# Linear attention with a channel mix on one core: pairs of heads share the handling of their maxima, q's exponentials are taken in one piece, the last tile is written in halves, and the instruction order is new

## The chip, the cores and the metric

The kernel runs on one core of a Trainium2 chip. The metric is the device time of one execution in microseconds (us), and lower is better. The engines of the core work side by side, each through its own list of instructions in order: TensorE (PE, matrix products), VectorE (DVE), ScalarE (ACT), GpSimd (POOL), and SyncE (SP), which here only issues transfers. They wait for one another through semaphores. SBUF is the on-chip memory. PSUM is where matrix products land.

## The reference, cut to what matters

Two operations follow each other. The first is a linear attention for 8 batches of 8 heads, 576 tokens each, head size 64. Its features are exponentials of a projection and of its negative, with the largest magnitude of each token taken off.

```
def phi(x):
    proj = einsum('bhsd,df->bhsf', x, w_phi)                 # 64 -> 128 features
    proj = proj - max(abs(proj), axis=-1, keepdims=True)
    return concatenate([exp(proj), exp(-proj)], axis=-1)     # 256 features
q_p, k_p = phi(q), phi(k)
kv  = einsum('bhsf,bhsd->bhfd', k_p, v);   z = sum(k_p, axis=2)
num = einsum('bhsf,bhfd->bhsd', q_p, kv);  den = einsum('bhsf,bhf->bhs', q_p, z)
attn = num / (den + 1e-06)
```

Its output, with the heads side by side as 512 columns, goes through a channel mix. That mix blends each token with the one before it and applies three products.

```
xk = mu_k * x + (1 - mu_k) * x_prev;  xr = mu_r * x + (1 - mu_r) * x_prev
k = maximum(xk @ w_k, 0)              # 512 -> 1024
out = sigmoid(xr @ w_r) * ((k * k) @ w_v)
```

## The kernel before

Heads are handled in pairs, one head in partitions 0 to 63 and the other in 64 to 127, so there are 32 pairs, four to a batch. A pair's tokens are cut into nine groups: eight are handled by the pair itself, and the ninth (the "edge") is handled for all pairs of a batch together. Nothing about the order is left to a scheduler. Each step is a named operation, and a long list of words called ORDER says in which sequence they are put out; since each engine works in order, this fixes the sequence on each engine. A word such as `mc5/ACT` puts the step mc of pair 5 on ScalarE, `kp1:0+2@2` puts kp of pair 1 into PSUM buffer 0 after two filler products, and a trailing `.d` marks the landing of a transfer.

The steps of one pair n, in the order of the data:

```
kp, qp   PE    projections of k and q (8 products each) into PSUM, 128 x 1024
rk, rq   DVE   per token the negated largest magnitude: nmk, nmq, 128 x 8 each
em       ACT   exp(+nmk), exp(-nmk): a factor for v (two instructions)
va, vb   POOL  v times that factor, once for each sign (some on DVE)
ea, eb   ACT   exp(+k), exp(-k), 128 x 1024 each
mh       POOL  nmq split into a high and a low bf16 part, in tile mhl (some on DVE)
mt, mc   PE, then DVE or ACT: mhl transposed, and copied out of PSUM as mT
qt       PE    q's projection once more, transposed, with mT added by selecting products
qa, qb   ACT   exp(+q), exp(-q)
kv, kc   PE, then ACT or DVE: kv and z, and their copy to SBUF
nd       PE    numerator and denominator
ra, rd   DVE   1/den, and num times it
xt or xz, xu   the result transposed (by PE, or by a transfer) and its shifted part copied
df       DVE or POOL   difference of neighbouring tokens
xa, xb   DVE   the blends xk and xr
```

For each batch the channel mix adds h (w_k product, 8 of them), rl (relu), sq (square), r (w_r product, 4), th (tanh), v (w_v product, 4), ob (product of the two branches) and so (store). An edge tile per two batches (he, rle, sqe, re, the, ve, obe, soe) does the same for the remaining tokens. The parts which the change touches:

```
        def em():
            for pn in range(2):
                nc.scalar.activation(vb[:, a, pn, 0:8, 64].rearrange("p (g r) -> p r g", r=2),
                                     s["nmk"].rearrange("p (r g) -> p r g", r=2), AF.Exp,
                                     scale=(1.0 if pn == 0 else -1.0))
        ... (cut)
        def mhx(eng):
            e = nc.vector if eng == "DVE" else nc.gpsimd
            nmv = s["nmq"].rearrange("p (a g) -> p a g", a=2)
            e.tensor_copy(mhv[:, 1, 0], nmv)
            e.tensor_tensor(mhv[:, 1, 1], nmv, mhv[:, 1, 0], op=ALU.subtract)

        def mt():
            s["pm"] = motile(("mo", "m" + N), "ps_m")
            nc.tensor.transpose(s["pm"][:, 0:64].bitcast(BF), mh, ident)

        def mc(eng):
            s["mT"] = small.tile([128, 128], BF, name="mT", bufs=BUFS["mT"])
            copy(eng, s["mT"], s["pm"][:, 0:64].bitcast(BF))
        ... (cut)
        def eq(pn):                                            # qa and qb
            def f():
                t = s[f"q{pn}"] = mid.tile([128, 2, 512], BF, name=f"q{pn}", bufs=BUFS["qpn"])
                for h in range(2):
                    nc.scalar.activation(
                        t[:, h, :].rearrange("f (g a p) -> f g a p", g=4, a=2),
                        s["qT"].rearrange("f a (g h p) -> f h g a p", g=4, h=2)[:, h],
                        AF.Exp, scale=(1.0 if pn == 0 else -1.0))
            return f
        ... (cut)
        # the edge tile's last steps
        def vm():
            s["v"] = ps = motile(("mo", f"ve{bp}"), "ps_ve")
            s["o"] = mm.tile([128, DM], FP, name="ob", bufs=BUFS["ob"])
            for fc in range(NFC):
                nc.tensor.matmul(ps, lhsT=s["kk"][:, fc, :], rhs=wv_bf[:, fc, :],
                                 start=(fc == 0), stop=(fc == NFC - 1))

        def ob():
            nc.vector.scalar_tensor_tensor(out=s["o"], in0=s["t"], scalar=1.0, in1=s["v"],
                                           op0=ALU.add, op1=ALU.mult)

        def so():
            for i in range(2):
                nc.sync.dma_start(out=out[b - 1 + i].rearrange("(p s) d -> s p d", s=R)[8 * (1 - i)],
                                  in_=s["o"][64 * i:64 * i + 64, :])
```

Of the kernel before, what the change touches and what calls it, by code (L numbers as in the profile page):

```python
# [8 lines left out]
FP = mybir.dt.float32  # L9
BF = mybir.dt.bfloat16  # L10
# [9 lines left out]
ones hk hq ident dve2 hk.d hq.d wphi wphi.d lk0.1 lk0.1.d lq0.1 lq0.1.d lv0.0/SP lv0.0.d lk0.2  # L20
lk0.2.d dve3 mus mus.d lq0.2 lq0.2.d lv0.1/POOL lv0.1.d lk0.0.d/DVE lk1.0 lk1.0.d lv0.2/SP lv0.2.d
lq0.0.d/DVE pt0.0:0+9@0 lq1.0 lq1.0.d pt0.1:1 pa0/DVE pb0/ACT tr0 lk1.2 lk1.2.d dve1 tp0.0:0+1@2
kp0:1 rt0.0 qp0:2 lq1.2 lq1.2.d rk0 ekt0.0 pt1.0:1+1@0 eme0.0 pt1.1:0 wk.0 wk.0.d pa1/ACT pb1/DVE
tr1 mhe0.0/POOL rq0 ea0 kp1:0+2@2 eb0 rk1 qp1:2+2@0 mh0/POOL wk.1 wk.1.d wk.d mt0:1 em0 tp0.1:1
mte0.0:0 ea1 mce0.0/DVE va0/POOL mc0/DVE rt0.1 pt2.0:0 pt2.1:1 pa2/DVE ekt0.1 vb0/POOL pb2/DVE tr2
eb1 qt0:1 rq1 pt3.0:1 eme0.1 lv1.0/POOL lv1.0.d pt3.1:0 qa0 qp2:0 pa3/DVE kv0:2 mh1/POOL pb3/DVE tr3
rq2 wr.0 wr.0.d qte0.0:1 kc0/ACT em1 tp0.2:2 mhe0.1/POOL qb0 mt1:0 rt0.2 kp2:0 va1/POOL rk2 mc1/ACT
ekt0.2 qp3:1 eqe0.0 vb1/POOL kp3:2+1@0 rq3 ea2 mte0.1:0 mhe0.2/POOL pt4.0:1+2@1 eb2 mce0.1/DVE kv1:1
pa4/DVE mh2/POOL rk3 qte0.1:0 eme0.2 pt4.1:1 mh3/POOL nd0:0 eqe0.1 wr.1 wr.1.d wr.d em2 mt2:0
kc1/DVE mc2/ACT pb4/DVE tr4 wv.0 wv.0.d ea3 qt1:1 ra0 rd0 pt5.0:1 va2/POOL eb3 pt5.1:0 pa5/DVE qp4:0  # L30
pb5/DVE tr5 wv.1 wv.1.d wv.d mte0.2:1 qa1 rq4 qp5:2 pt6.0:0 vb2/POOL qb1 mce0.2/DVE pa6/DVE qte0.2:1
qt2:0 lk2.0 lk2.0.d rq5 em3 eqe0.2 xt0:0 va3/POOL kp4:1 qa2 xf0/DVE xe0/DVE kv2:2 rk4 mh4/POOL mt3:0
pt6.1:1 kc2/ACT df0/POOL qb2 nd1:2 mc3/DVE pb6/DVE tr6 mt4:0 ea4 ra1 nd2:0 mc4/DVE lq2.0 lq2.0.d rd1
pt7.0:0 eb4 lv1.2/POOL lv1.2.d ra2 xt1:1 rd2 kp5:2 vb3/POOL xf1/ACT xe1/ACT qt3:1 rk5 pa7/ACT
pt7.1:1 mh5/POOL kv3:0 qa3 xa0 xt2:0 xb0 qb3 pb7/DVE tr7 xf2/ACT df1/DVE xe2/ACT tp1.0:1 kc3/DVE ea5
rt1.0 df2/POOL nd3:0+1@1 eb5 ra3 mhe1.0/POOL rd3 ekt1.0 qt4:2+4@1 xa1 xt3:0 eme1.0 mt5:1 xb1 mc5/ACT
xe3/ACT qt5:1+1@2 xa2 qa4 mte1.0:1 qp6:0 xb2 xf3/ACT qb4 df3/DVE mce1.0/DVE xa3 em5 qte1.0:1+2@0 em4
kp6:2 xb3 eqe1.0 va4/POOL rq6 r0.0:0+3@0 qa5 h0.0:1 vb4/DVE qb5 rk6 mh6/POOL kv4:0 tr2.0 tr2.0.d tr8
tr9 rl0.0/ACT vb5/POOL qp7:1 th0.0 h0.1:1 rq7 ea6 va5/POOL r0.1:0 kc4/DVE em6 rl0.1/ACT sq0.0/DVE
tr2.2 tr2.2.d tr10 tr11 kv5:0 vb6/DVE th0.1 kp7:1 eb6 mh7/DVE mt6:1 h0.2:0 rk7 sq0.1/POOL nd4:2  # L40
lk3.0 lk3.0.d mc6/DVE em7 rl0.2/DVE h0.3:1 kc5/ACT lv2.0/SP lv2.0.d vb7/POOL ea7 ra4 rd4 lv2.2/SP
lv2.2.d h0.4:0 eb7 rl0.3/DVE va7/POOL qp8:2 xt4:1 rl0.4/ACT rq8 nd5:1 va6/POOL sq0.3/ACT qt6:0
sq0.2/ACT xf4/DVE xe4/DVE tp2.0:2 lq3.0 lq3.0.d ra5 qa6 h0.5:0 rd5 sq0.4/POOL qb6 rt2.0 h0.6:1 lk4.0
lk4.0.d rl0.5/ACT kv6:1 rl0.6/DVE df4/POOL ekt2.0 qp9:0 kc6/DVE h0.7:0 rq9 sq0.5/ACT mhe2.0/POOL
mt7:1 kp8:2 rl0.7/ACT kv7:1 mc7/DVE mh8/POOL rk8 sq0.7/ACT kp9:0 sq0.6/POOL mte2.0:0 r0.2:1 eme2.0
kc7/ACT em8 xa4 nd6:1 mce2.0/ACT th0.2 xb4 v0.0:0 ea8 rk9 vb8/POOL eb8 v0.1:1 va8/POOL em9 ob0.0 ea9
ra6 so0.0 so0.0.d rd6 mh9/POOL eb9 lq4.0 lq4.0.d qte2.0:0 ob0.1 qp10:1 vb9/POOL eqe2.0 qt7:2 rq10
qp11:0 tr3.0 tr3.0.d tr12 tr13 r0.3:1 qa7 va9/POOL rq11 xt5:0 th0.3 kp10:1 mh10/POOL qb7 xe5/DVE
xt6:1 xf5/DVE rk10 kv8:0 df5/POOL tr3.2 tr3.2.d tr14 tr15 xe6/ACT mt8:0 nd7:2 kc8/ACT xf6/DVE
mc8/DVE ea10 mt9:1 xa5 qt8:0 v0.2:0 eb10 df6/DVE mc9/DVE ra7 xa6 em10 qa8 xb5 qt9:1 xb6 qb8 v0.3:1  # L50
ob0.2 va10/POOL qa9 rd7 vb10/POOL mt10:0 nd8:0 qb9 mc10/DVE ob0.3 xt7:0 ra8 kv9:2 mh11/POOL xf7/ACT
rd8 xe7/ACT kv10:1 kc9/ACT df7/DVE xz8 xz8.d qt10:0 kc10/ACT xa7 kp11:2 qa10 nd9:1 xb7 mt11:0 qb10
rk11 r1.0:1 mc11/ACT nd10:0 ra9 th1.0 rd9 r1.1:0 em11 ea11 ra10 vb11/POOL xz9 xz9.d rd10 kp12:1
th1.1 h1.0:1 rk12 va11/POOL eb11 so0.1 so0.1.d qp12:0 h1.1:0 rq12 ea12 xu8/POOL xz10 xz10.d df8/POOL
qt11:2 rl1.1/ACT rl1.0/DVE tp3.0:0 eb12 lv3.0/SP lv3.0.d h1.2:0 rt3.0 sq1.0/POOL so0.2 so0.2.d qa11
kp13:1 rl1.2/DVE mh12/POOL h1.3:1 tr4.0 tr4.0.d tr16 tr17 qb11 sq1.1/DVE sq1.2/POOL h1.4:0 rl1.3/DVE
ekt3.0 xa8 r1.2:1 eme3.0 sq1.3/DVE rl1.4/ACT qp13:0 rk13 mhe3.0/POOL kv11:2 tr4.2 tr4.2.d tr18 tr19
th1.2 em12 xu10/POOL mt12:0 h1.5:1 sq1.4/ACT xu9/POOL mc12/DVE va12/POOL kc11/DVE ea13 rq13 h1.6:0
vb12/POOL rl1.5/ACT nd11:2 rl1.6/DVE lv3.2/SP lv3.2.d em13 sq1.5/ACT qp14:0 xb8 mte3.0:1 h1.7:0 eb13
# [936 lines left out]
```

## Time and profile before

| Quantity | Value |
|---|---|
| Time, median of 3 runs | 287.51 us (286.61 to 288.0) |
| Span of the profiled execution | 286.8 us |
| DVE busy | 252.0 us, 88% of the span |
| ACT busy | 227.1 us, 79% |
| POOL busy | 156.7 us, 55% |
| Mean TensorE clock granted | 0.99 of full |

The page of the profile gives busy time for each engine, the span in 40 slices, the chain of work that ended last, and groups of equal instructions with their number, busy time and mean duration. In a group line, "out<-in" names the tile written and the tiles read, with partitions x elements and types; what stands after the second bar is the idle time of the engine just before them. The busy time of a group is less than number times mean where the ends of instructions overlap. A busy PE is not yet a full PE: its products are pipelined, so the number of products done in a stretch says more than the share of time.

### The profile page before, as it was taken

What the parts mean: (1) busy time and instruction counts of PE and PEld (TensorE: products, weight loads), DVE (VectorE), ACT (ScalarE), POOL (GpSimd) and SP (SyncE); (2) the same over time, 40 slices, a digit from 0 to 9 for tenths busy, and PEclk for the clock granted to TensorE, in tenths of its full rate; (3) what the DMA queues carried; (4) which work ended last, traced back from release to release, by engine and by line L of the source; (5) the groups of instructions that cost most, each with busy time, mean ns of one, the idle gap of its engine ahead of it and who ended that gap; (6) DMA issues with size and microseconds to landing.
All of it is one profiled execution on the core that took longest, in us unless ns stands there. A gap on an engine that the chain in (4) does not pass through costs nothing.

```text
span 286.8 us, 9054 instructions
## 1 busy us (share of the span) xinstructions
PE 267.4 (93%) x3729; PEld 154.4 (54%) x3729; DVE 252.0 (88%) x403; ACT 227.1 (79%) x488; POOL 156.7 (55%) x235
## 2 busy tenths in 40 slices
PE   6888889999999999999899989999999999999993
PEld 2556645556645656645556644565565646544541
DVE  6799999999999999999998999999999997873431
ACT  2699997999899899988879967799899979524710
POOL 8599637985567967644599446826356243300000
PEclk9799999999999999999999999999999999999998
DMA  7999989989768979995777959799831714345034
GB/s 170 219 240 248 208 196 221 193 140 197 107 86 208 209 126 199 172 209 125 230 109 103 225 160 162 173 136 187 145 49 41 197 39 98 28 94 126 22 74 110
DMA packets 65785, 42.89 MB, mean 150 GB/s; under 512 B 47120, under 2 KB 56720, under 8 KB 65744
## 3 DMA queue, kind: packets, MB, share of 16 engines
q1 hardware_dynamic: 54688, 28.19, 48.0%
q0 software_dynamic: 10912, 13.83, 27.8%
q8 instruction: 29, 0.48, 0.7%
q10 hardware_dynamic: 144, 0.29, 0.4%
q14 instruction: 12, 0.10, 0.1%
HBM read 33.62 MB, written 9.44 MB: 150 GB/s over the span
## 4 chain that ended last, share of the span: by engine, by line
PE 56%; DVE 21%; ACT 13%; DMA 4%; issue 4%; POOL 1%; SPq 0%; DVEq 0%; ACTq 0%
PE ps_h L803 16%; PE ps_v L836 12%; PE ps_r L822 8%; ACT k L600 5%; PE ps_kv L652 4%; DVE xr L728 4%; ACT q L639 4%; PE ps_nd L673 3%; DVE nmk L574 3%; DVE nmq L579 3%; DVE xk L728 3%; PE ps_q L561 2%; DMA wph_f<-in_w_phi_dram 2%; PE ps_k L561 2%; PE ps_qT L625 2%
## 5 line engine op out<-in xcount | busy, mean ns | idle before, releaser
L592 POOL TENSOR_TENSOR v<-vt,v 128x576 bf16<-128x576 f32 x57 | 72.4, 1284 | 42.9 <-ACT v L586 37.1
L639 ACT ACTIVATE q<-ps_qT 128x512 bf16<-128x512 f32 x128 | 68.1, 631 | 3.1 <-PE ps_qT L631 2.9
L600 ACT ACTIVATE k<-ps_k 128x1024 bf16<-128x1024 f32 x64 | 63.9, 1047 | 2.2 <-DVE nmk L574 1.9
L803 PE MATMUL ps_h<-xk,wk_bf 128*128 128x512 bf16 x256 | 61.6, 379 | 0.7 <-DVE mT L205 0.7
L836 PE MATMUL ps_v<-wv_bf,kk 128*128 128x512 bf16 x256 | 58.9, 379 | 0.0
L579 DVE TENSOR_REDUCE nmq<-ps_q 128x8 f32<-128x1024 f32 x32 | 38.7, 1214 | 1.9 <-PE ps_q L561 1.5
L836 PEld LDWEIGHTS <-kk 128*128 128x128 bf16 x256 | 24.2, 98 | 27.7
L574 DVE TENSOR_REDUCE nmk<-ps_k 128x8 f32<-128x1024 f32 x32 | 38.8, 1212 | 0.3 <-PE ps_k L561 0.2
L803 PEld LDWEIGHTS <-wk_bf 128*128 128x128 bf16 x256 | 22.9, 98 | 25.6 <-issue 1.3
L728 DVE SCALAR_TENSOR_TENSOR xr<-diff,mu_r_t,xs 128x576 bf16<-128x576 bf16 x32 | 33.8, 1065 | 0.0
L828 ACT ACTIVATE rt<-ps_r 128x512 bf16<-128x512 f32 x32 | 19.5, 609 | 17.6 <-PE ps_r L822 17.2
L209 ACT ACTIVATE krelu<-ps_h 128x512 bf16<-128x512 f32 x44 | 26.7, 606 | 7.6 <-PE ps_h L803 7.3
L822 PE MATMUL ps_r<-wr_bf,xr 128*128 128x512 bf16 x128 | 32.2, 379 | 0.2
L217 POOL TENSOR_TENSOR kk<-krelu 128x512 bf16<-128x512 bf16 x18 | 20.1, 1116 | 18.3 <-DVE krelu L211 11.1
L842 DVE SCALAR_TENSOR_TENSOR ob<-rt,ps_v 128x512 f32<-128x512 bf16 x32 | 21.5, 679 | 8.9 <-PE ps_v L836 7.5
L728 DVE SCALAR_TENSOR_TENSOR xk<-diff,mu_k_t,xs 128x576 bf16<-128x576 bf16 x32 | 28.1, 880 | 0.1
L685 DVE TENSOR_TENSOR x_sc<-ps_nd,rden 128x640 bf16<-128x640 f32 x32 | 26.2, 821 | 0.8
L722 POOL TENSOR_TENSOR diff<-xs 128x576 bf16<-128x576 bf16 x15 | 19.1, 1275 | 13.2 <-DVE mhl L610 4.1
L652 PEld LDWEIGHTS <-k 64*128 64x128 bf16 x1024 | 18.7, 94 | 7.0 <-issue 4.4
L561 PEld LDWEIGHTS <-qkT 64*128 64x128 bf16 x512 | 16.5, 95 | 11.0 <-issue 7.9
L652 PE MATMUL ps_kv<-v,k 64*128 64x65 bf16 x1024 | 21.9, 190 | 0.3 <-DVE x_sc L685 0.2
L673 PE MATMUL ps_nd<-kv,q 128*128 128x65 bf16 x512 | 21.4, 193 | 0.0
(102 smaller groups left out, 439.8 us busy)
## 6 DMA issues: line engine op xcount, KB each, us to landing
out_dram<-ob SPq DMA_DIRECT2D x72, 128.0 KB, 2.4
vt<-in_v_dram SPq DMA_DIRECT2D x12, 576.0 KB, 5.0
nat<-in_k_dram POOLq DMA_DIRECT2D x6, 576.0 KB, 8.5
nat<-in_q_dram POOLq DMA_DIRECT2D x6, 576.0 KB, 7.4
vt<-in_v_dram POOLq DMA_DIRECT2D x3, 576.0 KB, 11.5
wk_bf<-in_moe_w_k_dram POOLq DMA_DIRECT2D x2, 512.0 KB, 13.0
wv_bf<-in_moe_w_v_dram POOLq DMA_DIRECT2D x2, 512.0 KB, 10.1
nat<-in_k_dram POOLq DMA_DIRECT2D x3, 288.0 KB, 9.2
```

Of the source, the lines that this page charges most:

```text
L561: nc.tensor.matmul(ps[:, par, g * 128:(g + 1) * 128], lhsT=qkT[b][r, g0 + gg + g, :], rhs=wph[r, :], start=(g == 0), stop=(g == 3))
L574: nc.vector.tensor_reduce(s["nmk"], s["k"].rearrange("p a (g f) -> p (a g) f", f=128), axis=AX.X, op=ALU.max, apply_absolute_value=True, n ...
L579: nc.vector.tensor_reduce(s["nmq"], s["q"].rearrange("p a (g f) -> p (a g) f", f=128), axis=AX.X, op=ALU.max, apply_absolute_value=True, n ...
L592: (nc.vector if eng == "DVE" else nc.gpsimd).tensor_tensor(vb[:, a, pn, :, 0:64], vt[b, a // 2][:, a % 2, :].rearrange("p (s d) -> p s d", ...
L600: nc.scalar.activation(s[f"k{pn}"], s["k"].rearrange("p a (g f) -> p (a g) f", f=128), AF.Exp, scale=(1.0 if pn == 0 else -1.0))
L639: nc.scalar.activation(t[:, h, :].rearrange("f (g a p) -> f g a p", g=4, a=2), s["qT"].rearrange("f a (g h p) -> f h g a p", g=4, h=2)[:, ...
L652: nc.tensor.matmul(ps[:, hh, pn * 65:(pn + 1) * 65], lhsT=s[f"k{pn}"][r, c, :], rhs=vb[r, a, pn, 2 * g + par, :], start=(pn == 0 and c == ...
L673: nc.tensor.matmul(ps[:, bk, o * 65:(o + 1) * 65], lhsT=tail if sl < 2 else s[f"q{pn}"][:, h, G * 128:(G + 1) * 128], rhs=s["kv"][:, h, pn ...
L728: nc.vector.scalar_tensor_tensor(out=t[:, a, (b % 2) * S:(b % 2 + 1) * S], in0=s["d"], scalar=mu[:, a:a + 1], in1=xs[:, a, 0:S], op0=ALU.m ...
L803: nc.tensor.matmul(ps, lhsT=wk_bf[:, c, fc * 128:(fc + 1) * 128], rhs=xkt[bp][:, c, m0:m0 + 512], start=(c == 0), stop=(c == NDC - 1))
L822: nc.tensor.matmul(ps, lhsT=xrt[bp][:, c, m0 + ci * 128:m0 + (ci + 1) * 128], rhs=wr_bf[:, c, :], start=(c == 0), stop=(c == NDC - 1))
L836: nc.tensor.matmul(ps, lhsT=s["kk"][:, fc, ci * 128:(ci + 1) * 128], rhs=wv_bf[:, fc, :], start=(fc == 0), stop=(fc == NFC - 1))
```

## The change

From pair 4 on, two neighbouring pairs (4 and 5, 6 and 7, ...) form a unit. Their maxima land in one tile of 2 x 8 columns. One em, one mh, one mt and one mc then serve both. The transposed tile mT has room for both, because mhl had only half of its columns in use; qt selects rows 4j to 4j+3 for the pair j of the unit. Pairs 0 to 3 stay alone. The exponentials of q take all 1024 columns in one instruction, into a tile [128, 8, 128] instead of [128, 2, 512]; nd reads the same values from it. The last edge tile computes its w_v product, its ob and its store in two halves of 256 columns, and the final stores are issued by SP and ACT. The conditions by which the order was found are looser: h needs the xa of its batch alone, r the xb alone. The list ORDER is new from end to end, and with it the engine on which many steps run. The aim is less work on DVE, ACT and POOL and a shorter end.

```diff
+    ONE = 4
+        w = 1 if n < ONE else 2
+        u, c0 = (n, a) if w == 1 else (n - n % 2, a - a % 2)
+        first, last = n == u, n == u + w - 1
+        cp = cpl.setdefault(u, {})
... (cut: rk and rq write t[:, j, :] of a shared tile [128, 2, 8])
         def em():
             for pn in range(2):
-                nc.scalar.activation(vb[:, a, pn, 0:8, 64].rearrange("p (g r) -> p r g", r=2),
-                                     s["nmk"].rearrange("p (r g) -> p r g", r=2), AF.Exp,
+                nc.scalar.activation(vb[:, c0:c0 + w, pn, 0:8, 64].rearrange("p a (g r) -> p a r g", r=2),
+                                     cp["nmk"][:, 0:w, :].rearrange("p a (r g) -> p a r g", r=2), AF.Exp,
                                      scale=(1.0 if pn == 0 else -1.0))
... (cut)
-            nmv = s["nmq"].rearrange("p (a g) -> p a g", a=2)
-            e.tensor_copy(mhv[:, 1, 0], nmv)
-            e.tensor_tensor(mhv[:, 1, 1], nmv, mhv[:, 1, 0], op=ALU.subtract)
+            nmv = cp["nmq"][:, 0:w, :].rearrange("p k (a g) -> p k a g", a=2)
+            e.tensor_copy(mhv[:, 0:w, 0], nmv)
+            e.tensor_tensor(mhv[:, 0:w, 1], nmv, mhv[:, 0:w, 0], op=ALU.subtract)
... (cut: mt and mc once for each unit)
-                    nc.tensor.matmul(ps[:, par, g * 128:(g + 1) * 128], lhsT=sel[r, 4 + g, :],
-                                     rhs=s["mT"][r, :], start=False, stop=(g == 3))
+                    nc.tensor.matmul(ps[:, par, g * 128:(g + 1) * 128], lhsT=sel[r, 4 * j + g, :],
+                                     rhs=cp["mT"][r, :], start=False, stop=(g == 3))
... (cut)
-                for h in range(2):
-                    nc.scalar.activation(
-                        t[:, h, :].rearrange("f (g a p) -> f g a p", g=4, a=2),
-                        s["qT"].rearrange("f a (g h p) -> f h g a p", g=4, h=2)[:, h],
-                        AF.Exp, scale=(1.0 if pn == 0 else -1.0))
+                nc.scalar.activation(
+                    t.rearrange("f x (a p) -> f x a p", a=2),
+                    s["qT"].rearrange("f a (x p) -> f x a p", p=64),
+                    AF.Exp, scale=(1.0 if pn == 0 else -1.0))
... (cut: the last edge tile)
+        for hf in range(1 if bp < 3 else 2):
+            w = DM if bp < 3 else DM // 2
... (cut: ve, ob of w columns; stores)
+                e = "ACT" if hf == 1 and i == 1 else "SP"
... (cut: ORDER, new in all of its lines; its last words before and after)
-so7.2.d ve3:1 ob7.3 so7.3 so7.3.d obe3 soe3 soe3.d
+so7.2.d re3:0 ob7.3 so7.3 so7.3.d ve3.0:1 the3 ve3.1:0 obe3.0 soe3.0.a soe3.0.a.d obe3.1
+soe3.0.b soe3.0.b.d soe3.1.b soe3.1.b.d soe3.1.a soe3.1.a.d
```

The two lists put these steps on these engines. Only what differs is shown; all other steps keep their number and engine.

| Steps | before: DVE, ACT, POOL | after: DVE, ACT, POOL |
|---|---|---|
| em (two instructions each) | -, 32, - | -, 18, - |
| mh (two instructions each) | 4, -, 28 | 3, -, 15 |
| mc | 19, 13, - | 6, 12, - |
| mhe, mce (the edge's own) | 1+6, 4, 9 | 3+5, 5, 7 |
| va and vb | 7, -, 57 | 5, -, 59 |
| rl and rle | 21, 51, - | 19, 53, - |
| sq and sqe | 29, 22, 21 | 26, 28, 18 |
| kc | 7, 25, - | 13, 19, - |
| xe | 3, 5, - | 6, 2, - |
| xu (copy and clearing of one column) | 4, 4, 16 | 2, 12, 10 |
| pb, first cast of q | 7+1, 1+0, - | 6+0, 2+1, - |
| mt on PE | 32 | 18 |
| filler products on PE | 29 | 36 |

## The prediction

> **What bounds the kernel now.** I read the busy times by stage first, because one average over the span hides stages with different limits. The lines give, for each stretch of the span in us, busy time and number of instructions of PE, its weight loads, DVE, ACT and POOL, then the granted clock and the transfer share.
>
> ```profile
> 0.00:20.00 20.00, 15.40 (x178) 8.53 (x179) 15.78 (x39) 11.86 (x30) 15.69 (x31) 0.91 1.07 210
> 20.00:40.00 20.00, 16.78 (x359) 12.46 (x359) 19.82 (x37) 19.68 (x46) 13.82 (x25) 1.00 1.18 233
> 40.00:100.00 60.00, 57.99 (x918) 33.97 (x918) 59.06 (x90) 55.66 (x122) 44.01 (x58) 1.00 0.87 167
> 100.00:200.00 100.00, 95.60 (x1383) 55.39 (x1382) 96.44 (x140) 86.23 (x186) 61.70 (x90) 1.00 0.87 167
> 200.00:260.00 60.00, 59.53 (x769) 33.37 (x768) 52.99 (x86) 44.23 (x92) 21.48 (x34) 1.00 0.45 87
> 260.00:287.00 27.00, 22.14 (x126) 10.70 (x124) 7.95 (x15) 9.47 (x16) 0.00 (x0) 0.95 0.34 79
> ```
>
> DVE is 96 to 99% busy from 20 to 200 us, ACT nearly full from 20 to 40 us, and after 260 us only PE has work. PE's share looks high everywhere, so I counted its products by line in stretches of 20 us and multiplied them by their spacing when they run without a gap. The chain of waits shows 8 products of 512 columns in 1.73 us, 0.2165 each; the timeline gives kv 36 products in 0.57 us, nd 20 in 0.64 us, a projection of 8 in 0.22 us. The sum over the kernel is about 247 us. From 0 to 40 us it is 22.6 us (17.4 us lost), from 40 to 200 about 143 of 160 us (17 us lost), and from 200 to 282 us PE is full within a few per cent. So **DVE paces the kernel until about 200 us and PE after that**. A saving on DVE counts only while PE has gaps to close, at most 17 us in the middle.
>
> Next the groups of instructions, for what the change touches: number, busy time, mean in ns, and idle time before.
>
> ```profile
> L639 ACT ACTIVATE q<-ps_qT 128x512 bf16<-128x512 f32 x128 | 68.1, 631 | 3.1 <-PE ps_qT L631 2.9
> L600 ACT ACTIVATE k<-ps_k 128x1024 bf16<-128x1024 f32 x64 | 63.9, 1047 | 2.2 <-DVE nmk L574 1.9
> L728 DVE SCALAR_TENSOR_TENSOR xr<-diff,mu_r_t,xs 128x576 bf16<-128x576 bf16 x32 | 33.8, 1065 | 0.0
> L586 ACT ACTIVATE v<-nmk 128x8 bf16<-128x8 f32 x64 | 11.4, 263 | 4.1 <-DVE nmk L574 3.9
> L610 POOL CAST mhl<-nmq 128x8 bf16<-128x8 f32 x28 | 7.0, 250 | 6.8 <-DVE nmq L579 6.8
> L611 POOL TENSOR_TENSOR mhl<-nmq,mhl 128x8 bf16<-128x8 f32 x28 | 6.2, 222 | 2.3
> L205 DVE COPY mT<-ps_m 128x128 bf16<-128x128 bf16 x19 | 4.1, 215 | 0.2 <-PE ps_m L615 0.2
> ```
>
> The small operations are cheap: DVE's 19 copies of mT are 4.1 us of its 252. The two big reductions, 77 us, and the blends, 62 us, stay.
>
> Last the timeline of the end (start, duration):
>
> ```profile
> 280.25 1.89 PE L920 MATMUL ps_ve<-wv_bf,kke 128*128 128x512 bf16 x8
> 280.51 0.69 DVE L842 SCALAR_TENSOR_TENSOR ob<-rt,ps_v 128x512 f32<-128x512 bf16 x1 [1.09 <-PE ps_v L836]
> 282.24 0.69 DVE L924 SCALAR_TENSOR_TENSOR ob<-rt,ps_ve 128x512 f32<-128x512 bf16 x1 [1.04 <-PE ps_ve L920]
> 282.95 1.10 SPq L929 DMA_DIRECT2D out_dram<-ob  x2
> ```
>
> After the last products come one ob of 0.69 us, two stores issued one behind the other, 1.10 us, and 2.75 us until the span ends at 286.8.
>
> **What the Trainium skill says.** Its page "Perfetto Trace Analysis", section Identifying the Most-Contended Engine, takes occupancy as fair for the vector engines and not for matmuls; here PE's 267 us busy stand for 247 us of packed work, which agrees. "ScalarE: Activation LUTs", section What ACT_TABLE_LOAD costs, gives an activation with constants 186 ns plus 0.833 ns a column and 93 ns of overlap back to back: 612 ns for 512 and 1039 for 1024 columns, against 631 and 1047 in the trace. "SBUF — State Buffer", section Who interferes with whom, says that a DVE operation with two SBUF inputs and a GpSimd operation that reads SBUF exclude each other for a whole instruction. The trace agrees: xr takes 0.81 us in the end, where POOL is idle, and 1065 ns in the mean; one square beside POOL's v products took 1.44 us where its neighbours took 0.42.
>
> **The change part by part.**
>
> q in one piece. ACT runs two halves back to back in 1.09 us (timeline, x2), and a whole in 0.97 (k, x2 in 1.94). 64 x 0.12 is 7.7 us; by the busy times it is 68.1 less 63.9, 4.2. I take 6 us off ACT.
>
> Shared em. 28 instructions fewer, at 0.17 us each when back to back (x2 in 0.34): 4.8 us off ACT. Shared mh: 13 fewer on POOL at 0.250 + 0.222, 6.1 us, and one fewer on DVE, 0.8. Shared mt: 14 transposes fewer on PE at some 0.1 us (estimate from the gaps around them), 1.4 us, against seven more fillers at 0.2165, 1.5 us. PE's total doesn't move.
>
> Placement, with the means of the group lines. DVE loses 13 mT copies (2.8), the mh (0.8), two relus at 0.682 (1.4), three squares at 0.49 (1.5), two v products at 0.858 (1.7), two xu (0.8), and pb, a cast and one mTe (1.1): 10.1 us. It gains six kv copies at 0.417 (2.5), three xe at 0.444 (1.3) and two mhe (0.6): 4.4 us. Net **5.7 us off DVE**, some 2.3%. ACT, besides 6 and 4.8, loses six kv copies (2.3) and three xe (1.5), and gains six squares at 0.64 (3.8), eight xu at 0.44 (3.5), two relus (1.2) and two casts (1.2): net 4.9 us off ACT. POOL loses 6.1 (mh), 3.3 (three squares), 2.5 (six xu) and 0.9 (mhe), and gains 2.6 (two v products) and 0.7: net 9.5 us. Fewer POOL operations also block DVE less; I count nothing extra for it.
>
> How much of that is time? I added the means of DVE's operations in each list up to a mark, and PE's packed work from that mark on: if DVE paces the part before and PE the part after, their sum moves as the time does. At the first h of batch 4, DVE's sum goes from 190.3 to 184.7, times 0.915 (busy 252.0 over the sum of all means, 275) is 5.1 us less; PE's rest grows from 94.8 to 97.5, 2.7 more: net 2.4. At the first h of batch 5: 6.0 less, 4.3 more, net 1.7. At the last xb: 5.5 less, 1.7 more, net 3.8. I take **3.0 us**. The new list does DVE's work earlier but leaves PE more behind it, so only half of 5.7 arrives.
>
> The last tile in halves: the last ob shrinks from 0.69 to about 0.4 us (estimate, between the 0.42 us of a DVE reduction of 256 columns and half of 0.69), 0.3 us. The four stores are smaller, two engines issue them, but SP still has three; of the 1.10 us of issue I expect 0.3 to 0.5 back. In all **0.7 us**.
>
> More room before waits: in the new list 12 of the xu are on ACT, and between a result's transposing transfer and its xu there are mostly 9 to 23 us of DVE work, where before there were mostly 3 to 12. Before, POOL waited 9.9 us for these transfers, and DVE 1.8, but PE was mostly full then. I count **0.6 us**.
>
> The start stays: kp of pair 0 begins at 7.9 us, when w_phi has landed at 7.4, and its transfer is issued as before.
>
> Sum: 3.0 + 0.7 + 0.6 = 4.3 us, so 287.5 - 4.3 = **283.2 us**.
>
> **The rivals.** (1) Pairing makes a wait. mh now waits for both rq, em for both rk, and v of the first pair for the second pair's maximum. For it: before, POOL's v waited 37.1 us for em, so that path has little slack, and em stands 0.4 to 6 us of DVE work behind the second rk. Against it: POOL isn't the bound, and the list was arranged for the pairing. It would show as longer waits of kv on v, and give 287 to 290 us. (2) PE is the bound more widely than I think. Its 17 us in the middle may be the cost of small products between semaphores rather than of DVE; then the lighter DVE only idles, and the two small terms remain: 286 to 287. (3) The new order wins more than its sums. If fewer POOL operations shorten xr (mean 1065 against 810 alone, 8 us in total) by a third, and the start loses less than 17 us, the time falls by another 3 to 5 us, to 278 to 280. (4) ACT becomes the bound with its 12 xu, each able to hold up exponentials while a transfer is late; the distances speak against it. 286 to 289.
>
> **Range and chances.** The steps that can be counted, less DVE, ACT and POOL work and a shorter end, all point down. What can't be counted is how a wholly new order meets real durations, plus or minus 4 us. I put (3) a little above (1) and (2). Range **279.0 to 287.5**. Over 2% faster means below 281.8: **0.35**. Within 2%: **0.60**. Over 2% slower, above 293.3, needs rival 1 or 4 in force: **0.05**.
>
> **What would show it.** Right: DVE's busy time near 246 us, ACT's 222, POOL's 147; q as 64 instructions of about 1045 ns; PE full from before 200 us; the end after the last product shorter by 0.7 us. Wrong: DVE lighter with PE's gaps as long as before (rival 2), POOL's v or PE's kv waiting longer on em (rival 1), or ACT waiting on xs transfers (rival 4). If xr's mean falls towards 900 ns, rival 3 has come in.

## The result, and the profile after

The changed kernel takes **277.75 us** (median of 4 runs, 277.08 to 282.4) against 287.43 us (median of 4) for the kernel before: ratio 0.9657, 95% interval 0.9623 to 0.9692. It is 9.7 us faster, where the prediction said 4.3, and lies under the predicted range.

First the busy times by stage, in the same stretches as before: for each stretch busy time and number of instructions of PE, its weight loads, DVE, ACT and POOL, then the granted clock, the transfer share and GB/s. The span ends at 275.3.

```profile
0.00:20.00 20.00, 17.25 (x196) 9.60 (x198) 16.17 (x41) 14.33 (x34) 15.61 (x30) 1.00 1.05 214
20.00:40.00 20.00, 17.63 (x365) 12.93 (x365) 19.72 (x38) 19.99 (x43) 13.59 (x20) 1.00 1.17 233
40.00:100.00 60.00, 57.38 (x1000) 35.45 (x1015) 57.51 (x87) 57.75 (x101) 43.52 (x55) 1.00 1.03 187
100.00:200.00 100.00, 98.89 (x1446) 57.47 (x1463) 92.94 (x142) 89.66 (x166) 55.76 (x74) 1.00 0.87 170
200.00:260.00 60.00, 59.58 (x627) 32.62 (x631) 44.22 (x78) 38.54 (x69) 13.88 (x17) 1.00 0.32 69
260.00:287.00 27.00, 10.99 (x70) 6.01 (x68) 4.03 (x7) 2.80 (x5) 0.00 (x0) 0.97 0.25 59
```

Two things moved. Between 100 and 200 us DVE fell from 96.4 to 92.9 us and PE rose from 95.6 to 98.9: PE is now close to full a hundred microseconds earlier (by the table below it did 94.8 us of work in that stretch, before 89.2). And in the first 20 us PE did 196 products instead of 178 (at least five of the 18 more are fillers), at full clock.

How far PE is ahead shows when its work is added up by products, as the prediction did it (products of each line times their spacing, fillers left out; counted by the weight loads, since the later trace holds 3730 of these and only 3682 products):

| PE's work done at | 40 us | 100 us | 200 us | 240 us |
|---|---|---|---|---|
| before | 17.3 us | 68.5 | 157.7 | 195.5 |
| after | 18.3 us | 70.7 | 165.5 | 205.2 |
| lead | 1.0 us | 2.2 | 7.8 | 9.7 |

The start gives 1.0 us. Most of the lead grows between 100 and 200 us, where DVE had set the pace.

Next the groups that the change touches (number, busy time, mean ns, idle before).

```profile
L643 ACT ACTIVATE q<-ps_qT 128x1024 bf16<-128x1024 f32 x64 | 63.8, 1054 | 1.8 <-PE ps_qT L636 1.7
L732 DVE SCALAR_TENSOR_TENSOR xk<-diff,mu_k_t,xs 128x576 bf16<-128x576 bf16 x32 | 26.7, 839 | 0.1
L732 DVE SCALAR_TENSOR_TENSOR xr<-diff,mu_r_t,xs 128x576 bf16<-128x576 bf16 x32 | 25.6, 806 | 0.1
L591 ACT ACTIVATE v<-nmk 128x16 bf16<-128x16 f32 x28 | 5.8, 306 | 0.5 <-DVE nmk L579 0.5
L591 ACT ACTIVATE v<-nmk 128x8 bf16<-128x8 f32 x8 | 1.5, 261 | 0.0
L202 DVE COPY mT<-ps_m 128x128 bf16<-128x128 bf16 x6 | 1.3, 218 | 1.0 <-PE ps_m L620 1.0
L616 POOL TENSOR_TENSOR mhl<-nmq,mhl 128x16 bf16<-128x16 f32 (+1 forms) x15 | 3.2, 215 | 1.2
```

One whole exponential of q takes 1054 ns, as one of k does (1047). The 28 shared instructions of em, with twice the columns, take 306 ns in the mean, the 8 others 261 (263 before); in the subtraction of mh twice the columns add nothing (222 before). The line that the prediction did not count on is xr: the same 32 instructions on the same data, 1065 ns before and **806** now. The spread by tile (minimum/median/maximum ns) shows that it was no general slowness. Before:

```profile
L728 DVE SCALAR_TENSOR_TENSOR xr<-diff,mu_r_t,xs x32: 802/811/1864, 33.4 to 258.3; 128x576 bf16<-128x576 bf16 x32
```

After:

```profile
L732 DVE SCALAR_TENSOR_TENSOR xr<-diff,mu_r_t,xs x32: 754/810/819, 33.0 to 244.1; 128x576 bf16<-128x576 bf16 x32
```

The medians agree within 1 ns; only the long ones are gone. One of them in the timeline of the kernel before (start, duration):

```profile
60.14 2.94 POOL L592 TENSOR_TENSOR v<-vt,v 128x576 bf16<-128x576 f32 x2 [0.45 <-ACT v L586]
60.34 1.72 DVE L728 SCALAR_TENSOR_TENSOR xr<-diff,mu_r_t,xs 128x576 bf16<-128x576 bf16 x1
```

POOL has begun a v product 0.2 us earlier, and xr, which comes right behind xk on DVE, stands beside that product and takes 1.72 us, 0.91 more than its own time. I call this a **block**. POOL loses too: its two v products take 2.94 us there, where one without a block takes 1.17 (the median). In the trace of before I counted each blend, difference and square on DVE that took over 0.1 us more than its kind alone while POOL worked: 17 of them, 12.7 us too long in all. After: 3, with 1.35 us. In the new list xr follows directly behind xk in 6 cases instead of 14. The Trainium skill says in "SBUF — State Buffer", section Who interferes with whom, that a DVE instruction with two SBUF inputs contends with a GpSimd instruction that reads SBUF, and calls the ports that they share an exclusive lock. The trace agrees: the longest blocks (0.9 to 1.05 us) come near the length of a POOL operation (1.2).

Last the end, in the timeline (ACT issues the fourth store at 271.53):

```profile
269.13 1.91 PE L929 MATMUL ps_ve<-wv_bf,kke 128*128 128x256 bf16 x16
270.26 0.42 DVE L935 SCALAR_TENSOR_TENSOR ob<-rt,ps_ve 128x256 f32<-128x256 bf16 x1 [1.18 <-PE ps_ve L929]
270.71 1.75 SPq L942 DMA_DIRECT2D out_dram<-ob  x3
271.08 0.42 DVE L935 SCALAR_TENSOR_TENSOR ob<-rt,ps_ve 128x256 f32<-128x256 bf16 x1 [0.40 <-PE ps_ve L929]
```

From the end of the last products (271.04) to the end of the span it is 4.3 us; before it was 4.7 (282.14 to 286.8). The last ob is 0.27 us shorter, but SP still issues three stores one behind the other.

### The profile page after: what moved, and what is told of

Its sections match the earlier page's. It is cut to its first block, busy times and chain, and to the rows that moved or that the text cites. A ratio compares the mean times of both kernels' runs of the same rounds, so it can differ in the third digit from the quotient of the medians.

```text
span 275.3 us, 8865 instructions
## 1 busy us (share of the span) xinstructions
PE 261.7 (95%) x3682; PEld 154.1 (56%) x3730; DVE 234.6 (85%) x388; ACT 223.1 (81%) x413; POOL 142.4 (52%) x193
## 4 chain that ended last, share of the span: by engine, by line
PE 75%; DVE 8%; ACT 6%; issue 4%; DMA 3%; POOL 2%; SPq 0%; POOLq 0%; ACTq 0%
PE ps_h L810 19%; PE ps_v L843 17%; PE ps_r L829 9%; PE ps_nd L677 5%; PE ps_kv L656 5%; DMA qkT<-nat 3%; PE ps_he L897 3%; PE ps_ve L929 3%; PE ps_k L566 2%; PE ps_qT L630 2%; PE ps_q L566 2%; PE ps_qT L636 2%; ACT k L605 2%; DVE nmk L579 2%; PE ps_f L292 1%
## 5 line engine op out<-in xcount | busy, mean ns | idle before, releaser
L597 POOL TENSOR_TENSOR v<-vt,v 128x576 bf16<-128x576 f32 x59 | 69.8, 1203 | 33.5 <-ACT v L591 31.1
L605 ACT ACTIVATE k<-ps_k 128x1024 bf16<-128x1024 f32 x64 | 64.8, 1047 | 1.3 <-DVE nmk L579 1.3
L643 ACT ACTIVATE q<-ps_qT 128x1024 bf16<-128x1024 f32 x64 | 63.8, 1054 | 1.8 <-PE ps_qT L636 1.7
L810 PE MATMUL ps_h<-xk,wk_bf 128*128 128x512 bf16 x235 | 60.5, 380 | 1.2
L206 ACT ACTIVATE krelu<-ps_h 128x512 bf16<-128x512 f32 x48 | 28.8, 611 | 9.3 <-PE ps_h L810 9.3
L726 POOL TENSOR_TENSOR diff<-xs 128x576 bf16<-128x576 bf16 x15 | 20.2, 1346 | 28.8 <-ACT xs L706 12.7
L214 POOL TENSOR_TENSOR kk<-krelu 128x512 bf16<-128x512 bf16 x18 | 19.1, 1068 | 30.3 <-ACT krelu L206 26.6
L849 DVE SCALAR_TENSOR_TENSOR ob<-rt,ps_v 128x512 f32<-128x512 bf16 x32 | 21.7, 682 | 14.3 <-PE ps_v L843 12.7
L829 PE MATMUL ps_r<-wr_bf,xr 128*128 128x512 bf16 x116 | 31.1, 380 | 0.7
L732 DVE SCALAR_TENSOR_TENSOR xk<-diff,mu_k_t,xs 128x576 bf16<-128x576 bf16 x32 | 26.7, 839 | 0.1
L732 DVE SCALAR_TENSOR_TENSOR xr<-diff,mu_r_t,xs 128x576 bf16<-128x576 bf16 x32 | 25.6, 806 | 0.1
L566 PEld LDWEIGHTS <-qkT 64*128 64x128 bf16 x512 | 16.5, 94 | 11.0 <-issue 8.0
## 6 DMA issues: line engine op xcount, KB each, us to landing
wk_bf<-in_moe_w_k_dram POOLq DMA_DIRECT2D x2, 512.0 KB, 11.4
```

What stands on the lines that cost most here:

```text
L206: nc.scalar.activation(out_, in_, AF.Relu, scale=HALF)
L597: (nc.vector if eng == "DVE" else nc.gpsimd).tensor_tensor(vb[:, a, pn, :, 0:64], vt[b, a // 2][:, a % 2, :].rearrange("p (s d) -> p s d", ...
L605: nc.scalar.activation(s[f"k{pn}"], s["k"].rearrange("p a (g f) -> p (a g) f", f=128), AF.Exp, scale=(1.0 if pn == 0 else -1.0))
L643: nc.scalar.activation(t.rearrange("f x (a p) -> f x a p", a=2), s["qT"].rearrange("f a (x p) -> f x a p", p=64), AF.Exp, scale=(1.0 if pn ...
L732: nc.vector.scalar_tensor_tensor(out=t[:, a, (b % 2) * S:(b % 2 + 1) * S], in0=s["d"], scalar=mu[:, a:a + 1], in1=xs[:, a, 0:S], op0=ALU.m ...
L810: nc.tensor.matmul(ps, lhsT=wk_bf[:, c, fc * 128:(fc + 1) * 128], rhs=xkt[bp][:, c, m0:m0 + 512], start=(c == 0), stop=(c == NDC - 1))
```

## The experiments

Two answers could explain a gain bigger than the sum: less blocking of DVE by POOL, or something else in the new list or the shared code that the sums do not hold. In the texts on record, theory A is that the order pays through its few blocks, with what this would mean for each run. Theory B is that the cheaper code pays and the order only makes room for it. Theory C is that a list in a fixed order fits only the durations it was made for, so that any added work costs more than itself. So I asked three questions: which part of the change carries the gain, whether blocks cost time, and what else the list does. Each ratio is to the kernel before, run on the same chip; us are worked out from ratios times 287.4.

| Kernel | Median us | Ratio, 95% interval |
|---|---|---|
| order_only | 288.39 | 1.003 (1.0013 to 1.0046) |
| after_unshared | 287.79 | 1.001 (0.9991 to 1.003) |
| after_mt_each | 287.22 | 0.9998 (0.9976 to 1.002) |
| after_only_mt_shared | 281.04 | 0.9785 (0.9754 to 0.9815) |
| after_em_mh_each | 280.26 | 0.9743 (0.9711 to 0.9776) |
| after_q_halves | 279.69 | 0.9707 (0.9665 to 0.975) |
| before_q_whole | 292.43 | 1.0146 (1.0092 to 1.02) |
| before_halves | 287.85 | 1.0013 (0.9991 to 1.0034) |
| before_transpose_shared | 290.44 | 1.013 (1.0094 to 1.0165) |
| before_v_later | 289.09 | 1.0068 (1.0042 to 1.0093) |
| before_moved | 290.14 | 1.005 (1.0023 to 1.0076) |
| before_no_two_inputs | 281.21 | 0.9785 (0.9747 to 0.9823) |
| after_no_two_inputs | 278.47 | 0.9683 (0.9636 to 0.973) |
| before_one_input_even | 285.01 | 0.9865 (0.9831 to 0.99) |
| after_one_input_even | 282.44 | 0.9792 (0.9749 to 0.9835) |
| after_dve_dose | 297.94 | 1.0221 (1.0142 to 1.0301) |
| after_no_fillers | 281.31 | 0.9761 (0.9728 to 0.9794) |
| after_edge_later | 282.85 | none |

Medians are of all executions, while ratios leave out the disturbed ones, so the two can differ (most for the dose; for the edge moved later too few are left for a ratio).

### Which part carries it: parts taken out of the changed kernel

**The new list with all of the old code.** The steps of the second pair of each unit come back into the list, their transposes ahead of the next user of the PSUM buffer.

```diff
-    ONE = 4
+    ONE = 32                       # no pair shares
-... "mhl": 3, "nmq": 3, ... "mT": 3
+... "mhl": 4, "nmq": 4, ... "mT": 5
+mh5/POOL em5 mt5:0 mc5/ACT ... mt31 mc31      (put into ORDER)
 (q in halves of 512 and the last tile whole, as before)
```

> The new instruction order with the old code: pairs not shared, q's exponentials in two halves, the last tile whole (the second pair's mt and mc stand just ahead of the next use of their PSUM buffer, three small pools have one or two buffers more). Theory A (the order is what pays: after the change only 3 DVE operations stood blocked behind POOL where before there were 17, some 11 us of DVE time): most of the gain stays, 280 to 282 us, and xr keeps a mean near 810 ns. Theory B (the cheaper code pays, and the order only makes room for it): 284 to 287 us.

Measured 1.003, above both forecasts. The order with the old code brings nothing, although its blocks are gone (1.4 us by the same count) and DVE's busy time is 238.4 us instead of 252.0.

**The changed kernel with nothing shared** (only the first hunk above; q in one piece and the halves of the last tile stay).

> The changed kernel with the sharing undone (em, mh, mt and mc for each pair; q in one piece and the halves stay). Theory A: sharing is worth its sums only, 4.8 us of ACT, 3 of DVE, 6 of POOL and 14 transposes, none of it on an engine that is full for long, so 278.5 to 280.5 us. Theory B: 282 us or more.

Measured 1.001: nothing is left of the gain either. So the list needs some of the sharing. But which?

**Only mt and mc for each pair**, em and mh still shared:

```diff
-            cp["pm"] = motile(("mo", "m" + U), "ps_m")
+            s["pm"] = motile(("mo", "m" + N), "ps_m")
-            cp["mT"] = small.tile([128, 128], BF, name="mT", bufs=BUFS["mT"])
+            s["mT"] = small.tile([128, 128], BF, name="mT", bufs=BUFS["mT"])
+mt5:0 mc5/ACT ... mt7:1 mc7/ACT ...           (14 of each put into ORDER; "mhl": 4, "mT": 5)
```

> The changed kernel with mt and mc for each pair, the second pair's just ahead of the next use of their PSUM buffer; all else as changed. Theory A: the 14 added passes through the two single PSUM buffers cost 6 to 9 us, most of what was lost with the sharing undone: 284 to 287 us, with PE waiting for copies of mT. Theory B or C: the transposes are no worse than other added work, 279 to 282 us.

**Only em and mh for each pair**, mt and mc shared:

```diff
-                nc.scalar.activation(vb[:, c0:c0 + w, pn, 0:8, 64]...
+                nc.scalar.activation(vb[:, a, pn, 0:8, 64]...
-            e.tensor_copy(mhv[:, 0:w, 0], nmv)
+            e.tensor_copy(mhv[:, j, 0], nmv)
```

> The changed kernel with em and mh for each pair, 28 small instructions more on ACT and 24 + 4 more on POOL and DVE; all else as changed. Theory A: 4.8 us of ACT and 5 to 6 of POOL, of which 0.5 to 2 us reach the time: 278 to 280 us. Theory C: 281 us or more.

**q in halves** in the changed kernel (the old eq() and its tile):

> The changed kernel with q's exponentials in two halves, 64 instructions and 6 to 8 us of ACT more; all else as changed. Theory A: ACT is 96% and more busy from 20 to 100 us in the changed kernel, so 1 to 3 us reach the time: 279 to 281 us. Theory C: 282 us or more.

**The new list and the shared mt and mc alone**, all else as before (em and mh for each pair, q in halves, last tile whole):

> The new order with as much of the old code as fits into it: em and mh for each pair, q's exponentials in halves, the last tile whole; mt and mc alone stay shared. In the run with all of the old code, PE's products stood some 8 us waiting for copies of mT, at PSUM buffers into which I had put the second pair's mt. Theory A (the order is what pays, and those 8 us are of my placing): 279.5 to 282.5 us. Theory C (a list in a fixed order fits only the durations it was made for, and any added work costs more than itself): 284 us or more, without long waits on mT.

Taken out of the changed kernel, the shared transposes cost 0.9998 - 0.9657, 9.8 us; the shared em and mh 0.0086, 2.5 us; q in one piece 0.005, 1.4 us, with intervals that overlap, so that its share is not settled. The new list with shared transposes and nothing else new keeps **6.2 us**. That is not the saved work itself: 14 transposes are 1.4 us of PE and their copies about 3. What PE waits for tells why. The longest waits of PE in the kernel with mt and mc for each pair (who, for whom, us in total, times, longest):

```profile
PE ps_h L808 <- ACT mT L198: 2.0, 3, 1.0
...
PE ps_x L713 <- ACT mT L198: 1.4, 2, 0.8
PE ps_f L290 <- ACT mT L198: 0.9, 1, 0.9
PE ps_m L618 <- ACT mT L198: 0.8, 1, 0.8
```

Products of quite other parts (h, r, a result's transpose) wait for the copy of a transpose, because they take the PSUM buffer that the transpose held. The waits on mT's copies sum to 8.4 us (8.8 in each of the two runs with nothing shared); in the kernel before they were 0.7, and in the changed kernel none is listed. The new list was made for 18 transposes. Where I put the 14 others is a choice of mine, and a better place could cost less. So these runs show that the list loses its gain with the 14 transposes at these places, not that sharing is worth 9.8 us.

### Parts put into the kernel before

Here the old list stays, with only what each part forces.

**q in one piece:**

```diff
-                for h in range(2):
-                    nc.scalar.activation(t[:, h, :]..., s["qT"]...[:, h], AF.Exp, ...)
+                nc.scalar.activation(t.rearrange("f x (a p) -> f x a p", a=2),
+                    s["qT"].rearrange("f a (x p) -> f x a p", p=64), AF.Exp, ...)
```

> The kernel before with q's exponentials in one piece and nothing else. ACT loses 4 to 8 us of work. Theory A: DVE paces this kernel, so at most 1 us comes off, 286.5 to 287.5 us. Theory B: 283 to 285 us.

**The last tile in halves** (the last words of ORDER as in the diff of the change):

> The kernel before with the last tile in halves and nothing else. Both theories: the end after the last product is shorter by 0.3 to 0.8 us, 286.7 to 287.2 us.

**mt and mc shared** for 13 units:

```diff
+    ALONE = (0, 1, 2, 3, 14, 15)
-            s["pm"] = motile(("mo", "m" + N), "ps_m")
+            cp["pm"] = motile(("mo", "m" + U), "ps_m")
-mt5:1 mc5/ACT ... mt7:1 mc7/DVE ...           (13 of each taken out of ORDER; five mh earlier,
                                               mt and mc of 12 and 30 later)
```

> The kernel before with the transpose and its copy shared for 13 of the 14 units (em and mh still for each pair, some mh and mt moved a little to fit), 13 passes fewer through the two single PSUM buffers, 2.8 us of DVE copies fewer at most. Theory A: this list was made with those passes in it and PE waited for mT little, so 0 to 2.5 us come off: 285 to 287.5 us. Rival (the passes themselves pace PE): 4 us or more off, 283.5 us or less.

**The first transfers of v and q in the new order:**

```diff
-lv0.0/SP lv0.0.d ... lv0.1/POOL lv0.1.d ... lv0.2/SP lv0.2.d lq0.0.d/DVE
+lv0.0/POOL lv0.0.d ... lq0.0.d/ACT lv0.1/SP lv0.1.d ... lv0.2/SP lv0.2.d
```

> The kernel before with the first loads of v behind those of k and q, and the first cast of q on ACT, as in the changed kernel. w_phi then has less traffic beside it; in the changed kernel the first projection began at 6.9 us and not at 7.8. Theory A: some 0.9 us comes off the start and 0.5 to 1 us off the time, 286.5 to 287 us. Rival: the start is made up for later, no change.

None of them gains, and all four lie above what was expected. The halves do nothing that can be measured. q in one piece takes ACT from 227.1 to 224.0 us busy and makes the kernel **1.5% slower**. In the stretch from 100 to 120 us the loss can be seen. Before:

```profile
100.00:120.00 20.00, 19.48 (x337) 12.18 (x336) 19.62 (x29) 18.77 (x41) 14.34 (x23) 1.00 0.95 173
```

With q in one piece, that stretch and its timeline:

```profile
100.00:120.00 20.00, 17.31 (x247) 10.25 (x246) 15.10 (x20) 14.60 (x30) 12.54 (x18) 0.91 0.96 147
```

```profile
107.08 0.23 POOL L205 COPY xs<-xs 128x63 bf16<-128x63 bf16 x1 [4.19 <-DMA xs<-x_sc]
...
107.31 1.17 POOL L592 TENSOR_TENSOR v<-vt,v 128x576 bf16<-128x576 f32 x1
108.43 1.27 POOL L721 TENSOR_TENSOR diff<-xs 128x576 bf16<-128x576 bf16 x1
...
109.74 0.82 DVE L727 SCALAR_TENSOR_TENSOR xk<-diff,mu_k_t,xs 128x576 bf16<-128x576 bf16 x1 [3.37 <-POOL diff L721]
```

POOL comes to a copy 4.19 us before its transfer has landed, its later steps stand behind it, DVE's xk stands 3.37 us for the difference, and PE does 247 products instead of 337. A list in fixed order fits the durations for which it was made; less work in it can bring one engine to a wait too early. The shared transposes in the old list (1.013) keep 13.3 us of blocks, and PE waited 2.6 us for mh, of which two pairs must now be ready. This leaves open what sharing would do in a list of its own with the old placement.

The transfers in the new order cost 0.7%, and the granted clock falls. A window of that run's profiled execution:

```profile
10.00:20.00 10.00, 8.12 (x116) 5.43 (x116) 8.07 (x14) 7.50 (x22) 7.22 (x13) 0.67 1.16 255
```

In the kernel before, this stretch has 0.93. So moving these transfers by itself did not bring the gain of the new start.

### Do blocks cost time?

**Other places for ten blends.** In the old list ten moves, by a word or a few each, put blends that were blocked behind a neighbour with one input on DVE; nothing else changes.

```diff
-xb4 ... xb6 ... xb8 ... rk14 ... rd16 ... xb13 ... xb15 ... xb17 ... xb22 ... xa27
+(each a few words later or earlier in ORDER)
```

> The kernel before, code and engines untouched; ten of the blends that stood blocked behind POOL (xb of pairs 4, 6, 8, 13, 15, 17, 22 and xa of 10, 14, 27) are moved behind the next one to four DVE operations that have at most one SBUF input, so that POOL can finish beside those. Theory A: most of the 12.7 us of blocked DVE time goes, and as DVE paces the kernel 3 to 6 us come off: 281.5 to 284.5 us. Rival (a moved blend holds up h and r on PE, or other operations take the block over): 286 us or more.

A miss. The kernel became 0.5% slower, and the blocks went elsewhere (11.2 us instead of 12.7). The longest xr even grew to 2554 ns:

```profile
L725 DVE SCALAR_TENSOR_TENSOR xr<-diff,mu_r_t,xs x32: 806/812/2554, 31.8 to 257.3; 128x576 bf16<-128x576 bf16 x32
```

As the blocks stayed, it says nothing of their worth.

**Blends without a second SBUF input.** In both kernels the blends are left out: in their place a reduction over one element copies the difference, with one input. The values differ; the order and the sizes do not.

```diff
-                nc.vector.scalar_tensor_tensor(out=t[...], in0=s["d"], scalar=mu[:, a:a + 1],
-                                               in1=xs[:, a, 0:S], op0=ALU.mult, op1=ALU.add)
+                nc.vector.tensor_reduce(t[...], s["d"].unsqueeze(2), axis=AX.X, op=ALU.max)
```

> The kernel before with both blends replaced by a reduction over one element, which copies the difference (the blend with xs and mu is left out). It has one SBUF input in place of two. Theory A (DVE operations with two SBUF inputs stand blocked behind POOL): no xk or xr is longer than its fellows, DVE loses the 10 us that blocks cost there, and the time falls by 4 to 8 us beyond what the same edit does to the changed kernel. Rival (the blocks hide behind PE): the time falls by no more than in the changed kernel.

> The same edit in the changed kernel, where hardly a blend stood blocked: the control. Theory A: within 1.5 us of the changed kernel, by the difference of the two instructions' own durations. Rival: as much off as in the kernel before.

Both groups of the kernel before with this edit:

```profile
L728 DVE TENSOR_REDUCE xk<-diff 128x576 bf16<-128x576 bf16 x32 | 23.6, 740 | 0.7 <-POOL diff L722 0.6
L728 DVE TENSOR_REDUCE xr<-diff 128x576 bf16<-128x576 bf16 x32 | 23.5, 744 | 0.0
```

In the kernel before this brings 1 - 0.9785, **6.2 us**; in the changed kernel 0.7 us are lost, within the intervals. The same edit helps only where there are blocks. But a reduction takes 0.742 us where an unblocked blend takes 0.810; 64 times that is 4.4 us of lighter DVE work, which could be part of the 6.2.

**The same with DVE's work kept up**, by a small reduction behind each:

```diff
+                nc.vector.tensor_reduce(scr, s["d"][:, 0:8], axis=AX.X, op=ALU.max)
```

> The kernel before with each of the 64 blends replaced by a reduction with one SBUF input over the difference, as in the run with the blends replaced, and behind each a second small reduction over 8 columns, so that DVE's two operations together last about as long as an unblocked blend (0.81 us). The blends' values are left out. If the blocks behind POOL are what the blends cost, the gain of that earlier run (6.2 us) stays nearly whole: 281 to 283 us. If 4.5 us of lighter DVE work made a good part of it, and not the blocks, 284 to 287 us.

> Control: the changed kernel with the same replacement. It has 1.4 us of blocks left and DVE's busy time stays near 234 us: 277 to 279 us under each theory. If it slows to 280 or more, the added small reductions cost more than the blends took, and the pair tells less.

The pair of operations lasts as long as a blend. First an unblocked blend of the kernel before with the operation behind it, then a pair of this run with the operation behind it:

```profile
242.22 0.81 DVE L728 SCALAR_TENSOR_TENSOR xr<-diff,mu_r_t,xs 128x576 bf16<-128x576 bf16 x1
242.95 0.68 DVE L211 TENSOR_SCALAR krelu<-ps_h 128x512 bf16<-128x512 f32 x1
```

```profile
123.62 0.74 DVE L729 TENSOR_REDUCE xk<-diff 128x576 bf16<-128x576 bf16 x1
124.28 0.15 DVE L731 TENSOR_REDUCE scr<-diff 128x1 bf16<-128x8 bf16 x1
124.35 0.41 DVE L217 TENSOR_TENSOR kk<-krelu 128x512 bf16<-128x512 bf16 x1
```

Both times the next operation starts 0.73 us after the first. The records overlap, so a small reduction of 0.153 us adds only 0.07:

```profile
L731 DVE TENSOR_REDUCE scr<-diff 128x1 bf16<-128x8 bf16 x64 | 9.8, 153 | 0.0
```

With these 64, DVE's busy time rises from 239.2 to 243.2 us, by 4.0 and not by 9.8. So DVE's work was kept, and the kernel before still gains 1 - 0.9865, **3.9 us** (2.9 to 4.9 by the interval). That is what the blocks of the blends, 10.5 of the 12.7 us, cost there. The other 2.3 of the 6.2 us came from the lighter DVE work. By its ratio (283.5 us) the result lies between the two ranges of the expectation: both causes had a part.

The control did not stay level. It slowed by 0.0135, 3.9 us, with DVE busy for 234.0 us against 234.6 in the changed kernel. In its profiled execution PE waited 5.6 us for one transfer (1.1 in the changed kernel); whether this holds for its other executions is not shown. Measured against the controls, leaving out the second input helped the kernel before by 6.9 us more in the first pair of runs and by 7.8 in the second. So about 4 us is the cautious figure, and a larger worth is not excluded.

What remains as a reservation: the replaced blend no longer reads xs, so that tile may come free earlier. The controls have that too, and gained nothing. And since a block holds up POOL as well (its v products took 1284 ns in the mean before, 1170 with the blends replaced), the 3.9 us include what that is worth.

### What else there is

**A dose of DVE work in the changed kernel**: 11 reductions, some 13 us.

```diff
+                if i == 1 and n in (4, 6, 8, 10, 13, 15, 17, 18, 19, 22, 27):
+                    nc.vector.tensor_reduce(scr, sel, axis=AX.X, op=ALU.max)
```

> The changed kernel with a reduction of a constant tile, some 1.1 to 1.2 us of DVE, put behind xb of 11 pairs, those whose neighbourhood was blocked in the kernel before: about 13 us of DVE work given back. Theory A: the time rises by 5 to 9 us, to 283 to 287 us, since DVE paces the kernel until about 200 us. Rival (PE is the bound in the changed kernel and DVE has room): it rises by less than 3 us.

The ratio rose by 0.056, 16 us, more than the dose. In the profiled execution, the longest of the six (302.9 us), there are 9 blocks with 5.5 us, and PE waited 8.9 us for one transfer alone:

```profile
PE ps_e L467 <- DMA qkT<-nat: 8.9, 1, 8.9
```

So it does not show how much DVE's work matters by itself.

**Without fillers**: the first nine of the 36 stay, 27 go.

```diff
-tp0.0:0+1@2 ... pt1.0:1+1@0 pt1.1:1+2@2 ... xt3:0+7@1 ... kv5:0+1@2
+tp0.0:0 ... pt1.0:1 pt1.1:1 ... xt3:0 ... kv5:0
```

> The changed kernel without its fillers, except for the nine at the very start: 27 products of 512 columns, 5.8 us of PE, fewer, all before 60 us. Theory D (the fillers keep the granted clock up; in the run with v loaded later in the old order the clock fell to 0.67 between 10 and 20 us): the clock falls below 1.00 between 10 and 40 us and the time rises by 1 to 4 us, 279 to 282 us. Rival (they stand in gaps of PE and do nothing else): no change within 0.5 us, clock at 1.00.

It lost 0.0104, 3.0 us, although PE had 27 products less to do. In its windows the granted clock falls to 0.70:

```profile
10.00:20.00 10.00, 7.55 (x104) 5.17 (x103) 8.76 (x16) 9.51 (x22) 9.16 (x15) 0.70 1.16 262
...
40.00:60.00 20.00, 19.40 (x332) 10.82 (x331) 18.83 (x27) 18.75 (x34) 15.72 (x20) 0.92 0.73 151
```

The Trainium skill, "TensorE: Matmul & The Clock Gate", section Part 1: The HAM clock gate, says that the clock is throttled by default and that activity releases it. The windows agree. The fillers of the new list, seven more than before, hold the clock at 1.00 over its first 20 us; how much of the 3.0 us was there before (0.91 in the first 20 us) was not tried.

**The edge's projection of batch 3 later.** In the changed kernel one wait of PE on a transfer is left:

```profile
PE ps_e L466 <- DMA qkT<-nat: 1.1, 1, 1.1
```

```diff
-tp3.0:0        (where it stood)
+tp3.0:0        (behind eb11, five steps later)
```

> The changed kernel with one step moved: the edge projection of batch 3, which waited 1.1 us for the transposing transfer of q and k while PE stood still, goes behind kv of pair 10 and its neighbours. Theory A: 0.3 to 1 us off, 276.8 to 277.5 us. Rival: another product waits in its place, no change.

Its fastest execution took 277.57 us, no better than the changed kernel's median. Undecided; no gain is shown.

No version had a shorter median than the changed kernel.

## Why the prediction was wrong, step by step

- **What bounds the kernel: right as far as the runs go.** In the kernel before, with its blends replaced, 4.0 us more DVE work cost 2.3 us of time. In the changed one PE's lead grew with DVE's lighter work to 7.8 us at 200 us.
- **q in one piece: right in cost**, 1054 ns against the 1045 named. ACT's busy time is 223.1 us against 222. In time it is worth some 1.4 us, not settled, and in the old list it costs.
- **Shared em and mh: about right.** ACT's em went from 11.4 to 7.2 us (4.2; predicted 4.8), POOL's mh from 13.2 to 6.2 (7.0; predicted 6.1). They are worth 2.5 us of time.
- **Shared mt: 14 transposes and their copies, as counted.** Missed was what a transpose costs beside its own time, a turn of a shared PSUM buffer.
- **DVE's placement: this is the step that failed.** The prediction wrote: "Fewer POOL operations also block DVE less; I count nothing extra for it." DVE's busy time fell not by 5.7 to 246 us but by 17.4 to 234.6. Of that, 5.7 are the operations as counted in advance and 11.3 are blocks (12.7 less 1.35), together 17.0. In time the blocks are worth about 4 us, by the run of the kernel before with DVE's work kept (3.9). The missing part of the gain is 9.7 - 4.3, 5.4 us, so the blocks counted at nothing are the largest term of it that was found. That they brought as much in the changed kernel is inferred and not shown: with the old code the new order had as few blocks and gained nothing.
- **The reason given with it was wrong as well.** Fewer POOL operations are not what took the blocks away. POOL's long operations hardly became fewer (92 v products, squares and differences instead of 93), and with em and mh back for each pair, in the new order, 1.4 us of blocks are left. It is the order, which operation of DVE stands beside which of POOL. The blocks were to be seen in the profile before (8 us on xr), but only rival 3 had them, with a third; all 8 went.
- **The start: wrong in size.** The text held kp of pair 0 at 7.9 us. It begins at 7.01, and PE's lead at 40 us is 1.0 us, for which the sum has no term. The moved transfers alone, in the old list, lost 0.7%.
- **The end: 0.4 us in place of 0.7**, and nothing measurable when put in alone. More room before waits (0.6) was not seen apart from the rest, nor were the 3.0 us for the counted DVE work. So the parts of the sum are not confirmed one by one.
- **Rivals.** (1) did not come: POOL's v waited 31.1 us for em, where it was 37.1 before. (2) fell: PE's gaps closed. (4) fell: ACT waited 0.7 us for its xs transfers. (3) came, and beyond its range of 278 to 280.

What stays open: how the gain divides between the sharing and the order. The order without the sharing loses to PSUM waits partly of my placing, and the sharing in the old order loses to waits of its own. They were made for each other, and no run holds one of them at its best without the other.

## What to carry to other kernels

When a DVE operation with two SBUF inputs has a mean well above its minimum, list its long instances and what POOL does beside them: each block is time that a new order can give back without removing any work, and it belongs into the sum as a term of its own. It does not count at its full length: 10.5 us of blocks on the blends cost about 4 us of time here. And ten local moves in the old order only shifted them. Weigh an instruction also by what it holds, such as a turn of a scarce PSUM buffer, and not by its duration alone. And in a list of fixed order, try each saving with a list made for it; put into the old one, three savings here brought nothing or cost up to 1.5%.

## What the runs showed of the hardware that was not expected

A transposing transfer from nat to qkT mostly lands some 6 us after its issue, but in some executions one of them takes twice that, and PE waits for it. For the changed kernel, then for its run with the reductions in place of the blends, the time from issue to landing:

```profile
DMA to landing us min/median/max: 4.6/6.0/7.9
```

```profile
DMA to landing us min/median/max: 4.6/6.0/13.6
```

In the run with the dose the longest was 16.5 us; in the kernel before 8.5. The changed kernel comes to this transfer earlier, and one of its four executions took 282.4 us. Why the transfer is late at times, no run here shows.

Records of DVE's instructions overlap. The small reduction, 8 columns to one, has a record of 153 ns, but the operation behind it starts 0.07 us after it does, and 64 of them raised DVE's busy time by 4.0 us where their records sum to 9.8. What a small operation adds is read from start to start, not from its mean duration.
